# A linear-attention layer and its MoE block on one core: block-diagonal state, wider MoE units, twelve chunks transposed by DMA, every queue's order written out

## The chip, the core and the metric

The kernel runs on one core of a Trainium2 chip. The metric is the device time of one execution in microseconds. Time before: 212.34 us, the median of 3 runs (211.41 to 213.89). The profile is of one execution of its own.

The engines: PE (matrix products, with a separate path for loading weights, PEld), DVE (vector), ACT (scalar functions), POOL (a second vector engine without access to PSUM), and SP, which here only issues DMAs. PSUM, where PE writes, has 8 banks of 512 fp32 columns on each of 128 partitions.

## The reference

```python
def _attn_ref(r, k, v, w, u):          # each (4, 8, 768, 48); u (8, 48)
    state = np.zeros((B, H, D, D))
    for t in range(S):
        cur = np.einsum('bhd,bhe->bhde', u[None] * kt, vt)
        y[:, :, t] = np.einsum('bhd,bhde->bhe', rt, state + cur)
        state = wt[:, :, :, None] * state + np.einsum('bhd,bhe->bhde', kt, vt)
...
def _moe_ref(x, w_in, w_out):          # x (3072, 384), w_in (384, 2048), w_out (2048, 384)
    h = x @ w_in
    r = np.maximum(h, 0.0)
    g = r * r
    return g @ w_out
```

Attention's output y, its heads side by side, is the x of the second part. The output is (3072, 384) in fp32.

## The kernel before, in words

Attention is done in chunks of 128 time steps: 24 of them, 6 to each of the 4 batches. All 8 heads of 48 features lie side by side (384 columns); four pairs of heads share 128 partitions after a transpose, each head padded to 64. A chunk s runs through these helpers (lines are those of the profile):

- load_step (L71): w, r, k and v of the chunk, one DMA of 192 KB each. Rows of one head are 48 fp32 numbers, so the packets have 192 bytes. Seven buffers of each.
- lw_ (ACT, L151) takes log w. cum_ (PE, L178 to L181) makes the column sums of it (four matmuls of one column) and two cumulative sums, one strict for r and one negative and inclusive for k, in two PSUM banks. exp_ (ACT, L186, L187) exponentiates the column sums to a_c, and both cumulative sums in place.
- rd_ (DVE, L191) multiplies r and k by these decays. Eight 128x128 transposes follow, either on PE with a copy by DVE (tr_ L200, rkt_ L204), or, from chunk 18 on (DMA_FROM), as one DMA transpose issued from SP (dtr_, L208).
- p_ (PE, L223) makes the products of k and r for each head, with 64 rows each. pm_ (DVE, L229) masks them in two halves of 512 columns.
- su_ (PE, L238) multiplies decayed k and v for each head, eight matmuls of 48 columns; ts_ (DVE, L245, L247) adds the state S, sn_ (POOL, L251) multiplies by a_c. These tiles have 192 columns: two heads lie one above the other in the partitions.
- y_ (PE, L260, L268) multiplies the masked products by v and r by the state, again head by head, into two banks. ku_, qp_, vq_ (POOL, L159, L163, L171) and q_ (DVE, L167) make the diagonal term with u. ysb_ (DVE, L274) adds it. Three transposes give x transposed in the tile xT: yt_ and xt_ (PE L283, ACT L286), or dyt_ from chunk 18 on (a DMA transpose from SP, L213).

MoE works on blocks of one or two chunks of tokens (14 of them; the blocks of chunks 2, 3, 4 and 23 have one chunk). m1_ (PE, L301) makes one unit of 512 columns in one of two banks; rl_ (ACT, L308) takes 16 * relu to fp16, gt_ (DVE, L313) squares it. m2_ (PE, L320) accumulates an output tile of 128 tokens over 16 matmuls of 384 columns in the only bank for this; os_ (ACT, L325) scales it and store (SP, L329) writes it. Weights come in eight DMAs of 768 KB (L97, L103) and are cast by ACT and DVE (L110). Until MoE has begun, PE runs matmuls on zeros in its gaps (warm_, L334).

The order on every queue is made when the kernel is built: each operation stands in a plan with an engine, an assumed duration, a rank and its inputs, and make_order walks through it in assumed time. The engines then work through their queues in that order, each instruction waiting for its semaphores. So on SP a store or a transpose that waits for its input holds back all loads behind it. The 8 PSUM banks are divided as: two for cumulative sums and products, two for y, one for transposes and state updates, two for m1, one for m2.

Of the kernel before, what the change touches and what calls it, by code (L numbers as in the profile page):

```python
# [9 lines left out]
FP32 = mybir.dt.float32  # L10
FP16 = mybir.dt.float16
# [4 lines left out]

@with_exitstack
def kernel(
# [12 lines left out]
    PSUM = bass.MemoryType.PSUM  # L31

# [9 lines left out]
    NSTEP = B * NCH  # L42
    GW = 512
    RS = 16.0
    A_IN = 7
    HOP = .2
    PACE = 0.0
    DMA_FROM = 18
    LAG = 3.5

    nc.scalar.preload_act_table_set("natural_log_exp_and_others")

    consts = ctx.enter_context(tc.tile_pool(name="consts", bufs=1))
    weights = ctx.enter_context(tc.tile_pool(name="weights", bufs=1))
    stage_pool = ctx.enter_context(tc.tile_pool(name="stage", bufs=8))
    a_in = ctx.enter_context(tc.tile_pool(name="a_in", bufs=A_IN))
    a_mid = ctx.enter_context(tc.tile_pool(name="a_mid", bufs=2))
    a_small = ctx.enter_context(tc.tile_pool(name="a_small", bufs=3))
    gt_pool = ctx.enter_context(tc.tile_pool(name="gt", bufs=3))
    relu_pool = ctx.enter_context(tc.tile_pool(name="relu", bufs=3))  # L60
    o_pool = ctx.enter_context(tc.tile_pool(name="moe_out", bufs=3))

    ps_cp = ctx.enter_context(tc.tile_pool(name="ps_cp", bufs=1, space=PSUM))
    ps_y_pool = ctx.enter_context(tc.tile_pool(name="ps_y", bufs=1, space=PSUM))
    ps_tr_pool = ctx.enter_context(tc.tile_pool(name="ps_tr", bufs=1, space=PSUM))
    ps_m1 = ctx.enter_context(tc.tile_pool(name="ps_m1", bufs=2, space=PSUM))
    ps_m2 = ctx.enter_context(tc.tile_pool(name="ps_m2", bufs=1, space=PSUM))


    def load_one(dst, src, b, c):  # L70
        nc.sync.dma_start(  # L71
            out=dst, in_=src[b, :, c * C:(c + 1) * C, :].rearrange("h c d -> c h d"))

    raw = {}

    def load_step(step, part):
        b, c = divmod(step, NCH)
        if part == "w":
            raw["w", step] = a_in.tile([C, H, D], FP32, name="w_raw")
            load_one(raw["w", step][:], w, b, c)  # L80
        elif part == "r":
            raw["rk", step] = a_in.tile([C, 2, H, D], FP32, name="rk_raw")
            load_one(raw["rk", step][:, 0], r, b, c)
        elif part == "k":
            load_one(raw["rk", step][:, 1], k, b, c)
        else:
            raw["v", step] = a_in.tile([C, H, D], FP32, name="v_raw")
            load_one(raw["v", step][:], v, b, c)

    wi_sb = weights.tile([C, KT, DFF], BF16)  # L90
    wo_sb = weights.tile([C, NT, DM], BF16)
    xT = weights.tile([C, KT, B * S], BF16)
    w_st = {}

    def load_wi(g):
        w_st["i", g] = stage_pool.tile([C, KT, GW], FP32, name="w_st")
        nc.sync.dma_start(  # L97
            out=w_st["i", g][:],
            in_=moe_w_in[:, g * GW:(g + 1) * GW].rearrange("(a p) f -> p a f", p=128))

    def load_wo(g):
        w_st["o", g] = stage_pool.tile([C, 4, DM], FP32, name="w_st")
        nc.sync.dma_start(  # L103
            out=w_st["o", g][:],
            in_=moe_w_out[g * 512:(g + 1) * 512, :].rearrange("(a p) d -> p a d", p=128))

    def cast(eng, kind, g, j):
        dst = wi_sb[:, :, g * GW:(g + 1) * GW] if kind == "i" else wo_sb[:, g * 4:(g + 1) * 4, :]
        copy = nc.scalar.copy if eng == "A" else nc.vector.tensor_copy
        copy(dst[:, j], w_st[kind, g][:, j])  # L110

    u_bc = consts.tile([C, H, D], FP32)

    def load_u():
        nc.sync.dma_start(
            out=u_bc[:],
            in_=bass.AP(tensor=u.tensor, offset=u.offset,
                        ap=[[0, C]] + [list(x) for x in u.ap]))


    tri_strict = consts.tile([C, C], BF16)
    make_upper_triangular(nc, tri_strict[:], val=1.0, diag=False)
    tri_incl_neg = consts.tile([C, C], BF16)
    make_upper_triangular(nc, tri_incl_neg[:], val=-1.0, diag=True)
    ident = consts.tile([C, C], BF16)
    make_identity(nc, ident[:])
    ones_col = consts.tile([C, 1], BF16)
    nc.vector.memset(ones_col[:], 1.0)

    warm = consts.tile([C, 512], BF16)  # L130
    nc.vector.memset(warm[:], 0.0)  # L131

    NLW = 3
    lw_bufs = []
    for i in range(NLW):
        t = consts.tile([C, H, DP], BF16, name=f"lw_buf{i}")
        nc.gpsimd.memset(t[:], 0.0)
        lw_bufs.append(t)
    NRD = 3
    rdec_bufs = []  # L140
    for i in range(NRD):
        t = consts.tile([C, 2, H, DP], BF16, name=f"rdec_buf{i}")
        nc.vector.memset(t[:], 0.0)
        rdec_bufs.append(t)


    tiles = {}

    def lw_(s):
        lw = tiles["lw", s] = lw_bufs[s % NLW]  # L150
        nc.scalar.activation(lw[:, :, 0:D], raw["w", s][:], AF.Ln)  # L151

    def v_(s):
        v_bf = tiles["v", s] = a_mid.tile([C, H, D], BF16, name="v_bf", bufs=3)
        nc.scalar.copy(v_bf[:], raw["v", s][:])  # L155

    def ku_(s):
        ku = tiles["ku", s] = a_mid.tile([C, H, D], FP32, name="ku")
        nc.gpsimd.tensor_mul(ku[:], raw["rk", s][:, 1], u_bc[:])  # L159

    def qp_(s):
        qp = tiles["qp", s] = a_mid.tile([C, H, D], FP32, name="qprod")
        nc.gpsimd.tensor_mul(qp[:], raw["rk", s][:, 0], tiles.pop(("ku", s))[:])  # L163

    def q_(s):
        q = tiles["q", s] = a_small.tile([C, H], FP32, name="q")
        nc.vector.reduce_sum(q[:], tiles.pop(("qp", s))[:], axis=AX.X)  # L167

    def vq_(s):
        vq = tiles["vq", s] = a_mid.tile([C, H, D], FP32, name="vq", bufs=3)  # L170
        nc.gpsimd.tensor_mul(vq[:], raw["v", s][:],  # L171
                             tiles.pop(("q", s))[:, :, None].to_broadcast([C, H, D]))

    def cum_(s):
        lw = tiles.pop(("lw", s))
        cs = tiles["cs", s] = ps_cp.tile([C, 2, 512], FP32, name="cp")
        for p in range(HP):
            nc.tensor.matmul(cs[:, 0, DM + p:DM + p + 1], lw[:, 2 * p:2 * p + 2, :],  # L178
                             ones_col[:], start=True, stop=True)
        nc.tensor.matmul(cs[:, 0, 0:DM], tri_strict[:], lw[:, :, 0:D], start=True, stop=True)  # L180
        nc.tensor.matmul(cs[:, 1, 0:DM], tri_incl_neg[:], lw[:, :, 0:D], start=True, stop=True)  # L181

    def exp_(s):
        cs = tiles["cs", s]
        a_c = tiles["a_c", s] = a_small.tile([C, HP], FP32, name="a_c")
        nc.scalar.activation(a_c[:], cs[:, 0, DM:DM + HP], AF.Exp)  # L186
        nc.scalar.activation(cs[:, :, 0:DM], cs[:, :, 0:DM], AF.Exp)  # L187

    def rd_(s):
        rdec = tiles["rdec", s] = rdec_bufs[s % NRD]  # L190
        nc.vector.tensor_mul(  # L191
            rdec[:, :, :, 0:D], raw["rk", s][:],
            tiles.pop(("cs", s))[:, :, 0:DM].rearrange("p a (h d) -> p a h d", h=H))

    def tr_(s):
        rdec = tiles["rdec", s]
        ps_tr = tiles["tr", s] = ps_tr_pool.tile([C, 2, HP, C], BF16, name="tr")
        for i in range(2):
            for p in range(HP):
                nc.tensor.transpose(ps_tr[:, i, p, :], rdec[:, i, 2 * p:2 * p + 2, :], ident[:])  # L200

    def rkt_(s):
        rkT = tiles["rkT", s] = a_mid.tile([C, 2, HP, C], BF16, name="rkT")
        nc.vector.tensor_copy(rkT[:], tiles.pop(("tr", s))[:])  # L204

    def dtr_(s):
        rkT = tiles["rkT", s] = a_mid.tile([C, 2, HP, C], BF16, name="rkT")
        nc.sync.dma_start_transpose(  # L208
            out=rkT[:].rearrange("p i a t -> p (i a) t"),
            in_=tiles["rdec", s][:].rearrange("t i h d -> t (i h d)"))  # L210

    def dyt_(s):
        nc.sync.dma_start_transpose(  # L213
            out=xT[:, :, s * C:(s + 1) * C],
            in_=tiles.pop(("ysb", s))[:].rearrange("p h d -> p (h d)"))

    def p_(s):
        rkT = tiles["rkT", s]
        ps_p = tiles["p", s] = ps_cp.tile([C, 2, 512], FP32, name="cp")
        for p in range(HP):  # L220
            for e in range(2):
                rows = slice(e * DP, (e + 1) * DP)
# [291 lines left out]
```

## Time and profile before

| what | value |
|---|---|
| median of 3 runs | 212.34 us |
| the profiled execution, its own time | 213.79 us |
| span of that execution, first to last instruction | 212.0 us |
| mean granted clock of PE | 0.992 |
| start of the first MoE matmul | 21.22 us |
| last input load issued | 145.66 us |
| DMA queue: share of 16 engines over the span | 72.6% |
| packets under 512 bytes | 109200 of 116010 |

An engine's busy time is the union of its instructions' times; PE's is pipelined, so that a busy PE need not work at its peak. A wait is put down to what came last. DMA share is the mean busy share of the 16 DMA engines; it can be above 1 in a window when several packets overlap in one engine. A row of a timeline merges successive instructions of one kind: start, length, engine, line, operation, tiles, number.

### The profile page before, as it was taken

How to read it: one execution, taken by the hardware profiler on the slowest of the kernel's cores; microseconds unless marked ns; L12 is line 12 of the kernel's file. 1: busy time of each engine (PE TensorE's matmuls, PEld its weight loads, DVE VectorE, ACT ScalarE, POOL GpSimd, SP SyncE). 2: the span in 40 equal slices, each digit the busy share in tenths (PEclk: the TensorE clock that was granted, in tenths of full speed). 3: DMA queues.
4: the chain of work that ended last, by engine and by line, in shares of the span. 5: the costliest groups of instructions: out<-in, count | busy, mean ns of one | idle time of the engine just before them, and what ended most of it. 6: DMA issues, size and time to landing. Idle time of an engine off the chain costs nothing.

```text
span 212.0 us, 5530 instructions
## 1 busy us (share of the span) xinstructions
PE 194.2 (92%) x2162; PEld 138.1 (65%) x2166; DVE 147.3 (69%) x273; ACT 125.2 (59%) x249; POOL 83.5 (39%) x105
## 2 busy tenths in 40 slices
PE   7897997886999898989989999999999999999983
PEld 3354766554877665767767677777767777777751
DVE  3565795555799798979968999987786666533310
ACT  3353967644666667568477376787645753455530
POOL 5371320545655719747276376363712110000000
PEclk9999999999799999999999999999999999999999
DMA  7999899879975899599978978899444327111111
GB/s 129 202 324 340 200 383 219 170 160 192 181 152 117 174 163 195 107 200 167 178 166 160 204 165 159 155 205 150 101 107 108 62 63 108 56 40 37 39 46 68
DMA packets 116010, 32.61 MB, mean 154 GB/s; under 512 B 109200, under 2 KB 114448, under 8 KB 115984
## 3 DMA queue, kind: packets, MB, share of 16 engines
q1 hardware_dynamic: 115984, 32.25, 72.6%
q8 instruction: 17, 0.28, 0.6%
q14 instruction: 9, 0.07, 0.1%
HBM read 25.36 MB, written 4.72 MB: 142 GB/s over the span
## 4 chain that ended last, share of the span: by engine, by line
PE 44%; DMA 17%; SPq 12%; issue 8%; DVE 8%; POOL 5%; ACT 4%; DVEq 0%; POOLq 0%; ACTq 0%
PE m L320 18%; PE m L301 17%; SPq L71 9%; DMA v_raw<-in_v_dram 6%; DMA w_st<-in_moe_w_out_dram 4%; DMA w_raw<-in_w_dram 3%; DVE gt L313 3%; PE cp L223 2%; POOL qprod L163 2%; DMA rk_raw<-in_r_dram 2%; DVE pmT L229 2%; PE tr L200 2%; ACT o_sb L325 2%; DMA rk_raw<-in_k_dram 2%; SPq L97 1%
## 5 line engine op out<-in xcount | busy, mean ns | idle before, releaser
L301 PE MATMUL m<-xT,wi_sb 128*128 128x256 bf16 (+1 forms) x672 | 77.2, 260 | 3.6 <-ACT xT L286 2.5
L308 ACT ACTIVATE rl<-m 128x512 f16<-128x512 f32 x96 | 56.5, 598 | 39.9 <-PE m L301 39.0
L320 PE MATMUL m<-wo_sb,gt 128*128 128x384 bf16 x384 | 74.8, 326 | 1.8 <-ACT o_sb L325 0.8
L301 PEld LDWEIGHTS <-wi_sb 128*128 128x128 bf16 x672 | 59.0, 99 | 16.8 <-issue 4.7
L313 DVE TENSOR_TENSOR gt<-rl 128x512 bf16<-128x512 f16 x96 | 52.5, 562 | 19.7 <-ACT rl L308 19.5
L320 PEld LDWEIGHTS <-gt 128*128 128x128 bf16 x384 | 35.3, 98 | 20.7 <-DVE gt L313 1.5
L159 POOL TENSOR_TENSOR ku<-rk_raw,u_bc 128x384 f32<-128x384 f32 x24 | 24.3, 1012 | 45.7 <-DMA rk_raw<-in_k_dram 41.1
L229 DVE TENSOR_TENSOR pmT<-cp,tri_strict 128x512 bf16<-128x512 f32 x48 | 30.8, 682 | 4.6 <-PE cp L223 4.4
L191 DVE TENSOR_TENSOR rdec_buf<-rk_raw,cp 128x768 bf16<-128x768 f32 x24 | 22.8, 949 | 13.9 <-ACT cp L187 10.9
L171 POOL TENSOR_TENSOR vq<-v_raw,q 128x384 f32<-128x384 f32 x24 | 21.3, 889 | 15.6 <-DVE q L167 7.6
L163 POOL TENSOR_TENSOR qprod<-rk_raw,ku 128x384 f32<-128x384 f32 x24 | 25.3, 1052 | 1.1
L251 POOL TENSOR_TENSOR S<-t_state,a_c 128x192 bf16<-128x192 f32 x20 | 11.0, 552 | 24.5 <-DVE t_state L247 17.6
L187 ACT ACTIVATE cp<-cp 128x768 f32<-128x768 f32 x24 | 19.1, 797 | 1.0 <-DVE gt L313 0.2
L334 PE MATMUL m<-warm 128*128 128x512 bf16 x60 | 16.8, 409 | 1.3 <-DVE warm L131 1.2
L155 ACT CAST v_bf<-v_raw 128x384 bf16<-128x384 f32 x24 | 12.3, 510 | 9.6 <-DMA v_raw<-in_v_dram 9.2
L151 ACT ACTIVATE lw_buf<-w_raw 128x384 bf16<-128x384 f32 x24 | 12.5, 523 | 7.9 <-DMA w_raw<-in_w_dram 6.1
L167 DVE TENSOR_REDUCE q<-qprod 128x8 f32<-128x384 f32 x24 | 13.1, 546 | 5.3 <-POOL qprod L163 5.3
L325 ACT ACTIVATE o_sb<-m 128x384 f32<-128x384 f32 x24 | 11.8, 492 | 7.7 <-PE m L320 7.0
L274 DVE TENSOR_TENSOR y_sb<-vq,y 128x384 bf16<-128x384 f32 x24 | 13.1, 548 | 3.3 <-PE y L268 3.2
L204 DVE COPY rkT<-tr 128x1024 bf16<-128x1024 bf16 x18 | 12.3, 682 | 1.9 <-PE tr L200 1.9
L200 PE MATMUL tr<-ident,rdec_buf 128*128 128x128 bf16 x144 | 11.5, 225 | 1.2 <-DVE rdec_buf L191 1.0
L223 PE MATMUL cp<-rkT 64*128 64x128 bf16 x192 | 9.7, 221 | 2.1 <-DVE rdec_buf L191 1.9
(40 smaller groups left out, 136.1 us busy)
## 6 DMA issues: line engine op xcount, KB each, us to landing
w_raw<-in_w_dram SPq DMA_DIRECT2D x24, 192.0 KB, 4.3
rk_raw<-in_r_dram SPq DMA_DIRECT2D x24, 192.0 KB, 4.2
rk_raw<-in_k_dram SPq DMA_DIRECT2D x24, 192.0 KB, 4.2
v_raw<-in_v_dram SPq DMA_DIRECT2D x24, 192.0 KB, 4.1
out_dram<-o_sb SPq DMA_DIRECT2D x24, 192.0 KB, 2.0
w_st<-in_moe_w_in_dram SPq DMA_DIRECT2D x4, 768.0 KB, 8.2
w_st<-in_moe_w_out_dram SPq DMA_DIRECT2D x4, 768.0 KB, 8.2
u_bc<-in_u_dram SPq DMA_DIRECT2D x1, 192.0 KB, 4.3
```

Source lines behind the costliest of these rows:

```text
L71: nc.sync.dma_start(out=dst, in_=src[b, :, c * C:(c + 1) * C, :].rearrange("h c d -> c h d"))
L159: nc.gpsimd.tensor_mul(ku[:], raw["rk", s][:, 1], u_bc[:])
L163: nc.gpsimd.tensor_mul(qp[:], raw["rk", s][:, 0], tiles.pop(("ku", s))[:])
L171: nc.gpsimd.tensor_mul(vq[:], raw["v", s][:], tiles.pop(("q", s))[:, :, None].to_broadcast([C, H, D]))
L187: nc.scalar.activation(cs[:, :, 0:DM], cs[:, :, 0:DM], AF.Exp)
L191: nc.vector.tensor_mul(rdec[:, :, :, 0:D], raw["rk", s][:], tiles.pop(("cs", s))[:, :, 0:DM].rearrange("p a (h d) -> p a h d", h=H))
L229: nc.vector.tensor_mul(tiles["pmT", s][:, e], tiles["p", s][:, e].rearrange("p (a t) -> p a t", a=HP), tri_strict[:, None, :].to_broadcast ...
L301: nc.tensor.matmul(ps1[:, j, :], wi_sb[:, kk, n * 128:(n + 1) * 128], xT[:, kk, s0 * C:s0 * C + width], start=(kk == 0), stop=(kk == KT - 1))
L308: nc.scalar.activation(rl[:], tiles.pop(("m1", i, g))[:], AF.Relu, scale=RS)
L313: nc.vector.tensor_mul(tiles["gt", i][:, g * ng:(g + 1) * ng, :], rl[:], rl[:])
L320: nc.tensor.matmul(tiles["m2"][:], gt[:, n, mt * 128:(mt + 1) * 128], wo_sb[:, n, :], start=(n == 0), stop=(n == NT - 1))
L334: nc.tensor.matmul(ps[:], warm[:, 0:C], warm[:], start=True, stop=True)
```

## The change

The kernel is written anew around the same algorithm.

- *State.* S, its update and its product have 384 columns: 96 for a pair of heads, of which each head uses its own half, so that the state is block-diagonal. su and the state part of y are four matmuls of 96 columns on full rows. The zeros outside of the blocks come from am, the exponentials of the column sums written in two halves (ACT), with which POOL multiplies. The column sums moved from cum_ to su and are left out for a batch's last chunk.
- *One output bank.* y has one bank with the heads in order.
- *One cumulative sum.* From chunk 6 on, cum makes only the strict sum for r. ACT writes exp of the sum and of its negative (two operations of 384 columns); ACT also writes 1/w (iw), and POOL multiplies k by it (kd), which takes the place of the inclusive sum. Chunks 0 to 5 (the list TWO) keep two sums.
- *MoE units.* m1 has 1,024 columns in two banks; rl and gt have 1,024 columns. All blocks have two chunks (12 blocks). Output tiles alternate between two banks. The last tile is made, copied and stored in two halves of 192 columns.
- *Masks.* pm is one operation of 1,024 columns.
- *DMA transposes.* Chunks 12 to 23 use dtr and dyt (chunks 18 to 23 before).
- *Buffers.* One tile of 14 slots holds w, r, k, v of a chunk, or one of the eight weight loads. xT is a ring of 12 chunks. u is loaded as one row of 1.5 KB and spread by a matmul (ub, ubc) rather than loaded to 128 partitions.
- *Order.* The planner is gone. A string lists every operation, with the PSUM bank it uses; all queues follow it. Helpers for pairs of chunks are in the file too, and the order has none of them (PAIRS = 0).

The core of the diff:

```diff
+SLOTS = """
+s0:0 s1:1 s2:2 s3:3 i0:4 i1:5 i2:6 i3:7 s4:8 o0:9 o1:10 o2:11 o3:12 s5:13 s6:0 s7:1 s8:2 s9:3 s10:4 s11:5 s12:6 s13:7
+s14:8 s15:9 s16:10 s17:11 s18:12 s19:13 s20:0 s21:1 s22:2 s23:3
+"""
+ORDER = """
+Lk0 Lw0 warm7@7 Lr0 Lv0 lw0 Lw1 cum0@0 warm4@7 ex0 Lk3 rd0 v0 Lr1 tr0@3 lw1 su0@2 rkt0 Lk1 cum1@0 am0 ts0 Lu p0@4 ex1
+warm6@7 Lw3 sn0 pm0 Lw2 y0@2 warm1@7 rd1 ub@3 Lr3 warm3@7 ubc lw3 Lr2 tr1@3 ku0 cum3@0 rkt1 lw2 warm2@7 ku1 Lv4 ex3
+p1@4 warm10@7 pm1 qp0 Lv1 Li0 qp1 rd3 Lk2 q0 cum2@0 q1 tr3@3 Lv2 vq0 ex2 warm4@7 rkt3 ku3 v1 ysb0 p3@4 su1@3 vq1 pm3
+yt0@2 warm3@7 Li3 am1 xt0 qp3 ts1 ciA0.2 y1@2 Lv3 warm3@7 ciA0.1 sn1 ysb1 ciA0.0 q3 yt1@3 ku2 warm4@7 Li2 v4 rd2 xt1
+Li1 v2 qp2 ma0.0@4 q2 tr2@3 rl0.0 vq2 su2@2 rkt2 warm2@7 Lk4 am2 ciV3.1 p2@0 ciV3.2 warm2@7 v3 ciV3.0 ts2 vq3 su3@3
...
+Lk15 p11@0 gt4.2 su12@3 ma4.1@4 am12 pm11 qp14 dtr12 lw15 iw15 ku13 ts12 mb4.0.0@7 v13 st3.1 q14 rl4.1 y11@2 Lw14 kd13
+cum13@0 mb3.0.3 ysb11 ex13 Lr15 ma4.3@4 gt4.1 os3.0 rd13 qp13 yt11@3 mb4.0.1 rl4.3 sn12 Lr16 q13 p12@0 st3.0 kd15 xt11
...
+cum23@0 mb9.0.1 ysb21 ex23 mb9.1.1 dyt21 gt9.2 ma9.3@4 rd23 lw22 iw22 dtr23 cum22@0 ku22 mb9.1.2 rl9.3 mb9.0.2 kd22
+ex22 ma10.0@4 gt9.3 rd22 qp22 mb9.0.3 rl10.0 mb9.1.3 dtr22 q22 os9.0 su22@3 gt10.0 os9.1 p23@0 am22 ma10.1@4 ts22 vq22
+st9.1 pm23 st9.0 sn22 ma10.2@6 rl10.1 gt10.1 p22@0 rl10.2 y23@2 pm22 ma10.3@4 ysb23 gt10.2 y22@3 dyt23 rl10.3
+mb10.1.0@7 ysb22 mb10.0.0@6 gt10.3 dyt22 mb10.1.1 mb10.0.1 mb10.1.2 mb10.0.2 ma11.0@4 mb10.1.3 rl11.0 mb10.0.3 os10.1
+gt11.0 ma11.3@4 os10.0 st10.1 st10.0 ma11.1@6 rl11.3 gt11.3 ma11.2@4 rl11.1 gt11.1 mb11.1.0@7 rl11.2 mb11.0.0@6
...
+"""
+TWO = [0, 1, 2, 3, 4, 5]
+BUFS = {'rd': 4, 'lw': 3, 'rt': 4, 'pm': 3, 'v': 3, 'vq': 4, 'ys': 3, 'qp': 2, 'st': 3, 'rl': 3, 'gt': 3, 'o': 3}
...
+    def Lu():
+        nc.sync.dma_start(out=u_row[:], in_=bass.AP(tensor=u.tensor, offset=u.offset, ap=[[0, 1], [1, DM]]))
...
+    def iw(s):
+        nc.scalar.activation(single(s)[:, 0], buf(lw_b, s)[:, :, 0:D], AF.Exp, scale=-1.0)
+
+    def kd(s):
+        nc.gpsimd.tensor_mul(single(s)[:, 0], single(s)[:, 2], single(s)[:, 0])
...
+    def cum(s, bank):
+        if s in TWO:
+            nc.tensor.matmul(ps[:, bank, 0:DM], tri[:], buf(lw_b, s)[:, :, 0:D], start=True, stop=True)
+            nc.tensor.matmul(ps[:, bank + 1, 0:DM], ntri[:], buf(lw_b, s)[:, :, 0:D], start=True, stop=True)
+        else:
+            nc.tensor.matmul(ps[:, bank + 1, 0:DM], tri[:], buf(lw_b, s)[:, :, 0:D], start=True, stop=True)
...
+    def ex(s):
+        bank = held["cp", s]
+        if s in TWO:
+            nc.scalar.activation(ps[:, bank:bank + 2, 0:DM], ps[:, bank:bank + 2, 0:DM], AF.Exp)
+        else:
+            nc.scalar.activation(ps[:, bank, 0:DM], ps[:, bank + 1, 0:DM], AF.Exp, scale=-1.0)
+            nc.scalar.activation(ps[:, bank + 1, 0:DM], ps[:, bank + 1, 0:DM], AF.Exp)
...
+    def pm(s):
+        bank = held["p", s]
+        nc.vector.tensor_mul(buf(pm_b, s)[:].rearrange("p e a t -> p (e a) t"),
+                             ps[:, bank:bank + 2].rearrange("p e (a t) -> p (e a) t", t=C),
+                             tri[:, None, :].to_broadcast([C, 8, C]))
+
+    def su(s, bank):
+        for a in range(HP):
+            nc.tensor.matmul(ps[:, bank, a * 96:a * 96 + 96], buf(rd_b, s)[:, 1 - ri(s), 2 * a:2 * a + 2, :],
+                             buf(v_b, s)[:, 2 * a:2 * a + 2, :], start=True, stop=True)
+        for a in range(HP):
+            nc.tensor.matmul(ps[:, bank, DM + a:DM + a + 1], buf(lw_b, s)[:, 2 * a:2 * a + 2, :],
+                             ones[:], start=True, stop=True)
...
+    def am(s):
+        bank = held["su", s]
+        for e in range(2):
+            rows = slice(e * DP, (e + 1) * DP)
+            nc.scalar.activation(buf(am_b, s)[rows, :, e], ps[rows, bank, DM:DM + HP], AF.Exp)
...
+    def sn(s):
+        nc.gpsimd.tensor_mul(buf(st_b, s + 1)[:].rearrange("p (a e d) -> p a e d", a=HP, e=2),
+                             buf(ts_b, s)[:].rearrange("p (a e d) -> p a e d", a=HP, e=2),
+                             buf(am_b, s)[:, :, :, None].to_broadcast([C, HP, 2, D]))
...
+        if s % NCH:
+            for a in range(HP):
+                nc.tensor.matmul(ps[:, bank, a * 96:a * 96 + 96], rt1(s)[:, HP * ri(s) + a, :],
+                                 buf(st_b, s)[:, a * 96:a * 96 + 96], start=False, stop=True,
+                                 skip_group_check=True)
...
+    def rl(i, g):
+        bank = held["m1", i, g]
+        t = held["rl", i, g] = buf(rl_b, unit0[i] + g)
+        nc.scalar.activation(t[:], ps[:, bank:bank + 2].rearrange("p b n -> p (b n)"), AF.Relu, scale=RS)
+
+    def gt(i, g):
+        t = held.pop(("rl", i, g))
+        nc.vector.tensor_mul(buf(gt_b, i)[:, g * 1024:(g + 1) * 1024], t[:], t[:])
```

In the string, L followed by w, r, k or v is a load, Li and Lo are weight loads, ci and co casts (A on ACT, V on DVE), ma and mb the two MoE stages (block, unit or tile, quarter), os and st the output copy and store; the number after @ is the bank.

## The prediction

> **What bounds the kernel now.** I read the page first: engine shares, the 40 slices, the chain by engine. Then the windows by stage, then the waits, then the timeline around the first MoE matmul, the transposes and the end.
>
> ```profile
> PE 194.2 (92%) x2162; PEld 138.1 (65%) x2166; DVE 147.3 (69%) x273; ACT 125.2 (59%) x249; POOL 83.5 (39%) x105
> ...
> PE   7897997886999898989989999999999999999983
> ...
> DMA  7999899879975899599978978899444327111111
> ...
> PE 44%; DMA 17%; SPq 12%; issue 8%; DVE 8%; POOL 5%; ACT 4%; DVEq 0%; POOLq 0%; ACTq 0%
> ```
>
> PE is the fullest engine, and from the 28th slice (about 145 us) it has no gap, while DMA falls away there. Up to there DMA is just as full, and the chain mixes both. So there are two regimes: a front that the loads feed, and a back that is a backlog of MoE on PE.
>
> ```profile
> 0.00:60.00 60.00, 51.39 (x531) 33.49 (x536) 37.65 (x74) 34.02 (x68) 24.46 (x38) 0.97 0.96 226
> 60.00:140.00 80.00, 75.25 (x945) 55.66 (x945) 71.52 (x123) 52.70 (x110) 48.06 (x53) 1.00 0.88 165
> 140.00:185.00 45.00, 44.57 (x502) 32.49 (x500) 31.88 (x64) 27.15 (x52) 10.95 (x14) 1.00 0.52 104
> 185.00:212.00 27.00, 22.99 (x191) 16.44 (x189) 6.28 (x15) 11.32 (x20) 0.00 (x0) 1.00 0.13 45
> ```
>
> Columns after the length: busy PE, PE weight loads, DVE, ACT, POOL, granted clock, DMA share. PE idles 8.6 us in the first 60 us (DMA share 0.96) and 4.8 us from 60 to 140 (DVE 89% busy there). The loads end at about 150 us and 55 us of PE work are left.
>
> ```profile
> 21.22 1.47 PE L301 MATMUL m<-xT,wi_sb 128*128 128x256 bf16 x12 [1.04 <-ACT xT L286]
> ```
>
> ```profile
> 130.27 0.33 PE cp L223 x8
> 130.60 0.55 PE tr L200 x8
> 131.15 0.65 PE m L320 x4
> 131.80 0.66 PE m L301 x6
> ```
>
> The first fence, of the timeline, is the start of MoE. The second, rows of the chain (start, us, what), is the price list of PE when dense: 0.33 us for the products of a chunk, 0.55 for its eight transposes, 0.163 for a second-stage matmul, 0.109 for a first-stage one. By the timeline of the end, the last output tile waits 0.58 us (205.26 to 205.81) for its only bank.
>
> **PE before, as a sum.** MoE is 576 x 0.109 (a 128-column one counts half: twelve of them take 0.67) plus 384 x 0.163 = 125.4 us. Attention, from successive starts in the timeline at 142 to 151 us: two cumulative sums 0.33, column sums 0.11, products 0.33, state update 0.24, y 0.30, state part of y 0.20, transposes of y 0.17, of r and k 0.55. With 24, 24, 24, 20, 24, 20, 18 and 18 of them: 47.4. Total 172.8. The two chunks ahead of the first MoE matmul hold 4.2 of it. So 21.2 + 168.6 + 3.4 (last matmul to end) = 193.2, and 18.8 us of the 212.0 are idle, warm-up and slack after MoE began: about 10 before 60 us (6.2 idle, ten warm-up matmuls 2.1, and a clock of 0.83 in 50 to 60, 1.7), about 9 later.
>
> **What the change takes from PE.** 18 chunks with one cumulative sum: 18 x 0.16 = 2.9. Six more chunks transposed by DMA: 6 x (0.55 + 0.17) = 4.3. Block-diagonal state: 4 matmuls of 96 columns for 8 of 48, twice per chunk. No row has 96 columns. By columns it is 96/256 x 0.109 = 0.04 each, 0.16 for 0.24 and 0.20, a gain of 2.8 with the four dropped column sums (0.44); by the transposes of 128 columns it is 0.55/8 = 0.07 each, 0.28, a loss of 2.0. The eight matmuls of y, as full in rows and 48 wide, take 0.0375 each, so I stay near the columns: 0.045, a gain of 2.0. The MoE columns stay. Sum 9.2, PE total 163.6.
>
> **Start.** The first weights now come after 14 input loads, not 9. Under load an input load takes 1.0 to 1.1 us (issues spaced 0.95 to 1.1 us at 50 to 56 us); u shrinks to one row and saves one. In the trace the first weights were cast from 14.2 us on, so now at about 18.5, and 1.7 us of casts make it 20.2. The last of the 14, v of chunk 1, lands at about 17, and v in bf16, vq, y and its transposes put xT of chunk 1 at about 20 too. First MoE matmul 21 to 23, I take 22, but with 5.6 us of attention done rather than 4.2 (the order has chunks 0 and 1, the sums, transposes and products of 3 and the sums of 2 ahead of it). Left on PE: 158.0. **End.** Two output banks and a last tile in halves remove the 0.58 wait and a part of the copy (0.49): 3.4 becomes 3.2. Sum without idle: 22 + 158.0 + 3.2 = 183.2.
>
> **What idle stays.** The front is fed by the same bytes at share 0.96; of the 10 us there I keep 8. Later, against 9 us, several things move.
>
> DMA: 12 transposed chunks rather than 6.
>
> ```profile
> L208 SPq DMA_TRANSPOSE rkT<-rdec_buf x6: 1232/1237/2128, 142.2 to 174.0; - x6
> ```
>
> ```profile
> SPq L329 <- ACT o_sb L325: 50.9, 18, 4.9
> SPq L213 <- DVE gt L313: 11.6, 4, 4.0
> ```
>
> The first fence is the transpose of r and k: shortest, median and longest issue in ns; it lands 3.3 us after its issue, one of y 2.3. The second is the two largest of SP's own waits (us, times, longest): stores wait for their copies, transposes for DVE, and every load behind them waits too. Summing the DMA share by single microseconds between 155 and 189 us, a transpose of r and k costs about 1.45 us of all DMA engines (2.1 in 161 to 165, less 0.6 for the store in it), one of y 0.49. Six more chunks: 11.7 us. Shares up to 150 us sum to 138 us; less 13 stores and two transposes that is 127 for all loads. When the last transpose of r and k is issued in the new order, the queue has moved 126 + 18 x 0.6 + 11 x 1.45 + 10 x 0.49 = 158 us of DMA work. At share 1.04 (10 to 20 us) that is 154 us of clock, at the average 0.92 it is 174. PE work behind it is 24 us, which with the end puts the finish at 181 to 201. So DMA is nearly as tight as PE until the last chunks. The 14 input slots (7 before) let loads run further ahead, which is the cover.
>
> POOL: k times the inverse decay, 18 x 1.0; the state product has 384 elements for 192: between 0.55 and 0.89 each (rows of 192 and 384), I take 0.85, +6. Total 83.5 to about 107, 62% of the first 170 us; no bound. DVE: rkT -4, wider ts +4, mask product in one (1.29 for the pair, I take 1.2) -2, gt 48 x (0.75 free to 1.1) for 52.5: 129 to 146 against 147. ACT: inverse decay 18 x 0.52, split exp and am +6.5, wider rl -7, xT -3: about 131, 67%; no bound. A unit of 1,024 columns (1.31 on PE) frees its banks only after rl of 1.03 (0.176 for 4 columns, 0.598 for 512, so by the slope); between two units PE has on average two second-stage groups (1.3) and 0.8 of attention, so it is covered unless two ACT operations stand ahead.
>
> The row that speaks against it: gt takes 408 ns at best and 1,237 at worst, and the long ones lie beside POOL products.
>
> ```profile
> L313 DVE TENSOR_TENSOR gt<-rl x96: 408/425/1237, 22.8 to 203.2; 128x512 bf16<-128x512 f16 x96
> ```
>
> ```profile
> 121.77 1.85 DVE L313 TENSOR_TENSOR gt<-rl 128x512 bf16<-128x512 f16 x2
> ...
> 122.15 1.19 POOL L163 TENSOR_TENSOR qprod<-rk_raw,ku 128x384 f32<-128x384 f32 x1
> ```
>
> The excess over 0.42 is 52.5 - 40.3 = 12 us now; POOL is busy 49% of the first 170 us now and 62% then, so 12 x 62/49 = 15, on an engine with a tenth to spare. The Trainium skill (SBUF — State Buffer, Summary) says that a DVE operation with two SBUF inputs and a GpSimd operation that reads SBUF exclude each other, the second blocking fully; the rows agree. By it, an estimate of 48 x 0.62 x 0.5 us = 15.
>
> The Trainium skill (Advanced Engine Details and Errata, X-Bar Transpose) holds transposing DMAs as fast as regular ones. The rows differ: 256 KB in 1.45 us against 192 KB of a store in 0.6. By the rule six more chunks would cost an estimated 6.6 us, not 11.7, and the lower end would be 5 us earlier.
>
> So of the later 9 us I keep 6: coarser units, the DMA squeeze and gt give back part of what the tuned order could win. Span 183.2 + 8 + 6 = 197.2. The profiled execution took 213.79 for a span of 212.0; 197.2 + 1.8 = 199.0 is 0.931 of it, and of the median 212.34 that is 198.
>
> **Rivals.**
> 1. SP becomes the bound (slower). In chunks 12 to 22 SP issues per chunk 4 loads x 0.7 + 1.24 + 1.18 + a store 0.4 = 5.6 us, in order. PE's turn per chunk is 125.4/24 + 1.4 = 6.6. In the trace 12 transposes waited 26 us on SP (the row above, 6.2, 4.4 and 4.0), 2.2 each, with almost no load behind them. If they wait so with loads behind, a turn is 10 us and eleven turns lose 37. For: these waits, and 50.9 us at stores. Against: 14 slots, and the order can put a transpose where its input is ready. It ends slower once a transpose waits over 1.2 us on average (8.0 per turn, +15); I price it at 1.5: 198 + 11 x 2.0 = 220, less some prefetch, 216.
> 2. DVE and POOL hold each other: +8 us in the middle (60 to 140 is at 89% already): 206.
> 3. The order fits, and only the front's 8 us stay idle: 183.2 + 8 = 191.2 of span, 192.
> 4. DMA keeps its average of 0.92 and paces everything, and gaps of 7 to 10 us add up behind it: 201 + 9 = 210 to 213, no change.
>
> **Chances.** Forecast (194 to 202) 0.42; rival 3 0.18; rival 2 0.20; rival 4 0.07; rival 1 0.13. One per cent is about what a measurement of this kernel can tell from none: faster 0.82, same 0.05, slower 0.13. The range leaves out rival 1 and the lowest part of rival 3: 189 to 210; the forecast's own is 194 to 202.
>
> **What would show it.** Right: MoE starts at 21 to 23 us; PE has about 9 us less to do; the tail after the last matmul is near 3.2; DMA stays near 0.9 to 160 us and beyond; POOL near 107 busy. Rival 1: the chain full of SP between 90 and 165 us and DMA share well under 0.9 there. Rival 2: gt means over 1.1 us and DVE as releaser of PE's gaps. Wrong altogether: PE gaps of over 1 us before first-stage units, put down to rl, which would mean that the 1,024-column unit is too coarse for its one pair of banks.

## The result, and the profile after

The changed kernel takes 197.09 us (median of 4 runs, 195.81 to 197.90) against 213.12 us (4 runs) for the kernel before beside it: a ratio of 0.927 [0.917, 0.936]. A second measurement gave 196.97 us and 0.9223 [0.9192, 0.9253]. The forecast was 198 us. The profiled execution took 196.81 us for a span of 194.9 us, at a granted clock of 1.00.

The engines' shares, the slices and the chain by engine, from the page of the kernel after:

```profile
PE 182.9 (94%) x1823; PEld 129.6 (66%) x1823; DVE 140.1 (72%) x203; ACT 127.3 (65%) x249; POOL 110.7 (57%) x120
...
PE   6999988999998799899999999999998989999993
...
DMA  6999999996698999697998997799797799382202
...
q1 hardware_dynamic: 123794, 34.22, 83.7%
...
PE 55%; DVE 14%; DMA 8%; ACT 6%; issue 4%; SPq 1%; DVEq 0%; ACTq 0%
```

PE idles 12.0 us (194.9 - 182.9) where it idled 17.8, and does 11.3 us less. DMA no longer falls away at 145 us: input loads are issued until 162 us (145.7 before), and with the transposes they keep it full to about 165. SP has 1% of the chain (12% before), DMA half its former share, DVE nearly twice. The old border between a fed front and a dense back is gone.

The same windows as before, with the last one cut at the new end (columns: busy PE, PE weight loads, DVE, ACT, POOL, clock, DMA share, GB/s):

```profile
0.00:60.00 60.00, 56.05 (x501) 34.64 (x503) 43.47 (x75) 37.54 (x74) 28.93 (x40) 1.00 0.91 230
60.00:140.00 80.00, 76.54 (x833) 56.91 (x832) 66.98 (x88) 60.00 (x122) 63.23 (x62) 1.00 0.94 178
140.00:185.00 45.00, 43.45 (x435) 32.73 (x434) 27.54 (x39) 26.59 (x48) 18.52 (x20) 1.00 0.75 135
185.00:195.00 10.00, 6.84 (x63) 5.29 (x60) 2.08 (x3) 3.20 (x5) 0.00 (x0) 1.00 0.12 42
```

Idle of PE up to 60 us went from 8.6 to 4.0, although MoE starts later (23.33 us, 21.22 before); 60 to 140 went from 4.8 to 3.5. POOL has 63 of 80 us in the middle (48 before).

PE's timeline: the start of MoE, and the prices of y (masked products times v) and of the state part behind it.

```profile
23.33 1.47 PE L516 MATMUL ps<-xT,wi_sb 128*128 128x256 bf16 x12
...
54.15 0.36 PE L367 MATMUL ps<-v,pm 128*128 128x48 bf16 x8
54.35 0.33 PE L371 MATMUL ps<-st,rt 128*128 128x96 bf16 x4
54.52 0.33 PE L291 MATMUL ps<-lw,tri 128*128 128x384 bf16 x1
```

A row's own length overlaps the next, so prices are read between starts: eight matmuls of y cost 0.20 us, the four of the state 0.17. Before they stood so, in a chunk with a state part and then in the first chunk of a batch, which has none:

```profile
121.72 0.36 PE L260 MATMUL y<-v_bf,pmT 128*128 128x48 bf16 x8
122.02 0.27 PE L268 MATMUL y<-S,rkT 64*128 64x48 bf16 x8
122.22 0.34 PE L283 MATMUL tr<-ident,y_sb 128*128 128x128 bf16 x3
...
151.28 0.36 PE L260 MATMUL y<-v_bf,pmT 128*128 128x48 bf16 x8
151.48 0.24 PE L178 MATMUL cp<-ones_col,lw_buf 128*128 128x1 bf16 x4
```

So y fell from 0.30 to 0.20, which I had not priced, and the state part from 0.20 to 0.17. Without a state part behind it, y took 0.20 before as well, into the same two banks. The difference lies in its last matmul: the step from it to the next start is 0.115 us in all 20 chunks where matmuls on 64 rows (64*128) follow, and 0.025 in the four where matmuls on 128 rows do. The groups of relu and square in the page after (busy us, mean ns, idle before and its releaser):

```profile
L523 ACT ACTIVATE rl<-ps 128x1024 f16<-128x1024 f32 x48 | 49.0, 1023 | 24.7 <-PE ps L516 23.7
...
L527 DVE TENSOR_TENSOR gt<-rl 128x1024 bf16<-128x1024 f16 x48 | 42.4, 887 | 20.9 <-ACT rl L523 20.4
```

The square takes 42.4 us instead of 52.5, in half the operations.

### The profile page after: what moved, and what is told of

It is laid out like the page before. It is cut to its first block, busy times and chain, and to the rows that moved or that the text cites. A ratio compares the mean times of both kernels' runs of the same rounds, so it can differ in the third digit from the quotient of the medians.

```text
span 194.9 us, 4703 instructions
## 1 busy us (share of the span) xinstructions
PE 182.9 (94%) x1823; PEld 129.6 (66%) x1823; DVE 140.1 (72%) x203; ACT 127.3 (65%) x249; POOL 110.7 (57%) x120
## 3 DMA queue, kind: packets, MB, share of 16 engines
q1 hardware_dynamic: 123794, 34.22, 83.7%
## 4 chain that ended last, share of the span: by engine, by line
PE 55%; DVE 14%; DMA 8%; ACT 6%; issue 4%; SPq 1%; DVEq 0%; ACTq 0%
PE ps L542 23%; PE ps L516 21%; DMA rt<-rd 5%; DVE gt L527 3%; PE ps L326 3%; DVE rd L304 3%; DVE pm L332 2%; PE ps L367 2%; DMA raw<-in_r_dram 2%; PE ps L371 1%; DVE ts L356 1%; DVE ys L377 1%; DMA raw<-in_v_dram 1%; PE ps L312 1%; PE ps L291 1%
## 5 line engine op out<-in xcount | busy, mean ns | idle before, releaser
L516 PE MATMUL ps<-xT,wi_sb 128*128 128x256 bf16 x576 | 70.0, 273 | 1.6 <-DVE wi_sb L242 0.8
L542 PE MATMUL ps<-wo_sb,gt 128*128 128x384 bf16 (+1 forms) x400 | 70.9, 320 | 0.3 <-DVE gt L527 0.3
L523 ACT ACTIVATE rl<-ps 128x1024 f16<-128x1024 f32 x48 | 49.0, 1023 | 24.7 <-PE ps L516 23.7
L516 PEld LDWEIGHTS <-wi_sb 128*128 128x128 bf16 x576 | 55.0, 98 | 11.7 <-DVE wi_sb L242 1.4
L527 DVE TENSOR_TENSOR gt<-rl 128x1024 bf16<-128x1024 f16 x48 | 42.4, 887 | 20.9 <-ACT rl L523 20.4
L270 POOL TENSOR_TENSOR qp<-raw,u_bc 128x384 f32<-128x384 f32 x24 | 27.0, 1128 | 11.3 <-DMA raw<-in_k_dram 8.5
L332 DVE TENSOR_TENSOR pm<-ps,tri 128x1024 bf16<-128x1024 f32 x24 | 29.2, 1218 | 5.6 <-PE ps L326 5.6
L359 POOL TENSOR_TENSOR st<-ts,am 128x384 bf16<-128x384 f32 x20 | 18.7, 937 | 22.8 <-DVE ts L354 8.3
L273 POOL TENSOR_TENSOR qp<-raw,qp 128x384 f32<-128x384 f32 x24 | 26.6, 1111 | 3.4 <-DMA raw<-in_r_dram 2.9
L279 POOL TENSOR_TENSOR vq<-raw,q 128x384 f32<-128x384 f32 x24 | 20.7, 862 | 13.3 <-DVE q L276 13.3
L304 DVE TENSOR_TENSOR rd<-raw,ps 128x768 bf16<-128x768 f32 x24 | 22.8, 949 | 6.4 <-ACT ps L297 2.5
L551 ACT ACTIVATE o<-ps 128x384 f32<-128x384 f32 (+1 forms) x25 | 11.7, 476 | 8.8 <-PE ps L542 8.7
```

The source lines that it names most:

```text
L270: nc.gpsimd.tensor_mul(buf(qp_b, s)[:], single(s)[:, 2], u_bc[:])
L273: nc.gpsimd.tensor_mul(buf(qp_b, s)[:], single(s)[:, 1], buf(qp_b, s)[:])
L279: nc.gpsimd.tensor_mul(vq_b[:, s % BUFS["vq"]].rearrange("p (h d) -> p h d", h=H), single(s)[:, 3], buf(q_b, s)[:, :, None].to_broadcast([ ...
L304: nc.vector.tensor_mul(buf(rd_b, s)[:, :, :, 0:D], single(s)[:, x:x + 2], ps[:, bank:bank + 2, 0:DM].rearrange("p a (h d) -> p a h d", h=H))
L332: nc.vector.tensor_mul(buf(pm_b, s)[:].rearrange("p e a t -> p (e a) t"), ps[:, bank:bank + 2].rearrange("p e (a t) -> p (e a) t", t=C), t ...
L359: nc.gpsimd.tensor_mul(buf(st_b, s + 1)[:].rearrange("p (a e d) -> p a e d", a=HP, e=2), buf(ts_b, s)[:].rearrange("p (a e d) -> p a e d", ...
```

## The experiments

The theory on trial was the one of my forecast: PE's work plus the gaps that remain sets the end. The rivals: DMA or SP paces the kernel; DVE and POOL hold each other; and, as it turned out, the order rather than the parts is what gains. Ratios are to runs of the kernel before on the same chip, with 95% intervals.

| run | us, median | ratio to before |
|---|---|---|
| after, again | 196.97 | 0.9223 [0.9192, 0.9253] |
| e1: two cumulative sums again | 197.21 | 0.9229 [0.9196, 0.9263] |
| e2: chunks 12 to 17 transposed by PE | 203.41 | 0.9503 [0.9464, 0.9542] |
| e3: relu and square in halves | 209.40 | 0.9797 [0.9767, 0.9827] |
| e8: relu alone in halves | 197.09 | 0.9262 [0.9198, 0.9325] |
| e9: square alone in halves | 208.94 | 0.9778 [0.9685, 0.9871] |
| e5: after, long load rows | 194.72 | 0.9107 [0.9043, 0.9170] |
| e6: before, long load rows | 208.31 | 0.9739 [0.9677, 0.9802] |
| e4: before, DMA transposes from chunk 12 | 220.32 | 1.0283 [1.0203, 1.0364] |
| e10: before, wide square | 216.78 | 1.0173 [1.0110, 1.0237] |
| e7: all parts of after, order by the old planner | 211.49 | 0.9879 [0.9780, 0.9977] |
| e11: as e7, DMA transposes from chunk 18 | 209.68 | 0.9843 [0.9778, 0.9908] |

**The change once more (a0).**

> The changed kernel as it is, as the yardstick of this group: 197 us, 0.92 to 0.94 of the kernel before, by every theory.

It measured 196.97 us, as expected.

**e1: the inclusive sum back on PE.**

```diff
-TWO = [0, 1, 2, 3, 4, 5]
+TWO = list(range(24))
 # ORDER: every iw and kd taken out
```

> Two cumulative sums in all chunks; the inverse decay (ACT, 18 x 0.52) and its product with k (POOL, 18 x 1.03) are gone. Theory (PE work sets the end): PE gets 18 x 0.16 = 2.9 us more, so about 200 us, although POOL falls by 18 and ACT by 13. Rival (DVE, POOL and ACT feed PE too slowly): no slower than the changed kernel, 193 to 197.

```profile
PE 185.8 (95%) x1841; PEld 131.7 (67%) x1841; DVE 138.8 (71%) x203; ACT 118.3 (60%) x213; POOL 90.9 (46%) x102
```

PE is busy 2.9 us longer, exactly as priced, and the time does not move (+0.2 us, the intervals lie on each other): the rival's range came, not my 200 us. POOL has 19.8 us less and ACT 9.0 less, the mean square falls from 887 to 832 ns, and PE's idle time from 12.0 to 10.2 us. What PE saves by the single sum, PE gives back in gaps. As part of this order, that edit is worth nothing, and a sum of PE's work alone does not forecast it.

**e2: six chunks transposed by PE again.**

```diff
 # ORDER, for each chunk N of 12 to 17, at the same place
-dtrN
+trN@b rktN
-dytN
+ytN@b xtN
```

> Chunks 12 to 17 transposed by PE, at the place in the order where the DMA transposes stood. Theory (PE work): PE gets 6 x (0.45 + 0.18) = 3.8 us more, so about 201 us, although the DMA queue has 11.7 us less to do. Rival (DMA or SP paces the second half): faster than the changed kernel, 190 to 196.

It costs 6.4 us (203.41 against 196.97). PE is busy 4.9 us more (187.8), and its idle time grows from 12.0 to 14.3 us: the copies are back on DVE and ACT, in an order that was written without them. The windows of e2:

```profile
0.00:60.00 60.00, 56.05 (x496) 34.56 (x497) 43.13 (x75) 37.23 (x74) 28.72 (x39) 1.00 0.90 229
60.00:140.00 80.00, 73.96 (x825) 55.94 (x823) 63.27 (x88) 58.11 (x120) 56.01 (x55) 1.00 0.69 141
```

The DMA share from 60 to 140 us falls from 0.94 to 0.69, yet PE is busy 2.6 us less in this stretch. That refutes DMA or SP as what paces this order.

**e3, e8, e9: halves again.** MoE units stay at 1,024 columns; relu, square or both go in two operations of 512.

```diff
-        nc.scalar.activation(t[:], ps[:, bank:bank + 2].rearrange("p b n -> p (b n)"), AF.Relu, scale=RS)
+        for b in range(2):
+            nc.scalar.activation(t[:, b * 512:(b + 1) * 512], ps[:, bank + b], AF.Relu, scale=RS)
...
-        nc.vector.tensor_mul(buf(gt_b, i)[:, g * 1024:(g + 1) * 1024], t[:], t[:])
+        for b in range(2):
+            cols = slice(b * 512, (b + 1) * 512)
+            nc.vector.tensor_mul(buf(gt_b, i)[:, g * 1024:(g + 1) * 1024][:, cols], t[:, cols], t[:, cols])
```

> Units of 1,024 columns on PE as they are, but relu and square each in two operations of 512. ACT gets 48 x (2 x 0.598 - 1.023) = 8.3 us more. Theory (PE work): hidden, 196 to 199 us. Rival (ACT and DVE near the path, the wide operations are the gain): 201 us or more.

> The changed kernel with only relu in two operations of 512 columns (ACT +8 us); the square stays at 1,024. Theory formed after the first runs (what halving costs is DVE: every square is one more operation that POOL can lock out): 197 to 199 us. Rival (the longer turn on ACT, whose end frees the banks): 203 or more.

> The changed kernel with only the square in two operations of 512 columns; relu stays at 1,024. Theory (DVE and the lock): DVE about 17 to 20 us busier, 205 to 209 us. Rival (ACT's turn): 197 to 199.

All 12 us come from the square (e9: 208.94); the relu in halves is neutral (e8: 197.09). My first theory, which had e3 hidden at 196 to 199 us, was wrong; the ranges for e8 and e9, written after it, came. The tile of the squares, in after and then in e3 (shortest, median and longest ns):

```profile
L527 DVE TENSOR_TENSOR gt<-rl x48: 675/693/1490, 29.1 to 187.6; 128x1024 bf16<-128x1024 f16 x48
```

```profile
L530 DVE TENSOR_TENSOR gt<-rl x96: 407/426/1245, 29.5 to 200.2; 128x512 bf16<-128x512 f16 x96
```

In e3 the squares keep DVE busy for 63.4 us in place of 42.4. By the medians 96 x 0.426 - 48 x 0.693 = 7.6 of these 21.0 us is the plain cost of more operations; the other 13.4 is length that single ones gain. In after, the 16 squares with no POOL operation beside them take 675 to 693 ns, the 32 others up to 1,490; in e3 it is 407 to 426 for 38, and up to 1,245 for 58. The timeline of e3 shows where:

```profile
99.26 1.00 POOL L273 TENSOR_TENSOR qp<-raw,qp 128x384 f32<-128x384 f32 x1
99.29 4.65 DVE L530 TENSOR_TENSOR gt<-rl 128x512 bf16<-128x512 f16 x4
...
100.21 1.18 POOL L270 TENSOR_TENSOR qp<-raw,u_bc 128x384 f32<-128x384 f32 x1
...
101.35 1.18 POOL L264 TENSOR_TENSOR raw<-raw 128x384 f32<-128x384 f32 x1
...
102.49 1.17 POOL L273 TENSOR_TENSOR qp<-raw,qp 128x384 f32<-128x384 f32 x1
...
103.87 1.21 DVE L332 TENSOR_TENSOR pm<-ps,tri 128x1024 bf16<-128x1024 f32 x1
...
105.13 0.37 PE L367 MATMUL ps<-v,pm 128*128 128x48 bf16 x8 [2.42 <-DVE pm L332]
...
105.73 1.49 PE L545 MATMUL ps<-wo_sb,gt 128*128 128x384 bf16 x4
...
107.01 2.46 PE L516 MATMUL ps<-xT,wi_sb 128*128 128x256 bf16 x12
```

Four squares take 4.65 us, 1.16 each, the very step of the POOL operations (1.14 between their starts, 1.00 when undisturbed): the two engines alternate, one operation each. The mask product behind them is late, and PE stands for 2.42 us. A wide square pays such a turn at most once per 1,024 columns (1.49 - 0.69 = 0.80), a halved one twice. This is what the Trainium skill (SBUF — State Buffer, Summary: rules for kernel authors) describes as the second one blocking until the first is done; the rows agree with it.

The last two rows show a second cost. Four second-stage matmuls take 1.28 us between starts where they take 0.65 elsewhere: for 3.4 us from 105.6 us the granted clock is half. Such a stretch stands at 71.5 us too, and after has none. An estimate is 1.7 us for each, half its length. In e9 the execution at a clock of 0.999 took 206.81 us, and two at 0.982, which is two such stretches, 208.66 and 209.22. So about 2 of the 12 us go with the clock. How much of the other 10 is the lock and how much an order written for other durations, these runs do not part.

**e5, e6: loads with rows of 1,536 bytes.** Inputs are read as contiguous rows, so other elements land in the tiles; the number of bytes stays.

```diff
+ in_=bass.AP(tensor=src.tensor, offset=src.offset + s * C * DM, ap=[[DM, C], [1, DM]])
```

> The changed kernel with the input loads of w, r, k and v reading as many bytes in rows of 1,536 bytes (other elements than the reference's, so the output is not the reference's). It shows how much of the time the short packets hold. Theory (PE work, with a front fed by DMA): MoE starts about 4 us earlier and idle in the front goes, 187 to 191 us. Rival (DMA paces all of it): 183 or less. Rival (DMA is hidden throughout): 195 or more.

> The kernel before with the same edit of its loads (output not the reference's). Theory: its front idles 10 us and starts MoE late for the same reason, 202 to 206 us. Rival (its gaps came from its order and banks, not from DMA): 209 or more.

```profile
q1 hardware_dynamic: 37778, 34.22, 64.0%
```

The queue of e5 has less than a third of the packets and 64.0% of the span instead of 83.7%, and the kernel gains 2.3 us, 1.1 of it in the start of MoE (22.26 for 23.33 us). I had expected 187 to 191 us; 194.72 lies by the rival's 195, of a hidden DMA. The kernel before gained 5.5 us, less than I expected too (202 to 206). So the old one was paced by loads in part, as its chain said, and the new one hardly is.

**e4: the DMA transposes alone, in the kernel before.** One number, `DMA_FROM` 18 to 12; the planner makes the order anew.

> The kernel before with one constant changed: DMA transposes from chunk 12 on, its own planner ordering all. Theory (PE work): PE has 3.8 us less, so 209 to 210 us. Rival (the DMA queue, 92% full up to 150 us, and SP in order): the same or slower, 213 to 220.

```profile
PE 31%; DMA 27%; SPq 15%; DVE 9%; ACT 7%; issue 6%; POOL 3%; ACTq 0%; DVEq 0%; POOLq 0%
```

6.5 us slower, just past the rival's range; my theory had it faster. The same edit that is worth 6.4 us in the new kernel (e2) costs as much in the old one. Here DMA and SP take 42% of the chain (29% before), SP's waits ahead of transposes grow from 26.2 to 31.7 us, and the loads of w go from 3% to 12% of the chain. That fits transposes that hold back loads behind them in SP's queue; it was not tried apart. The trace also has two stretches at half clock where before has one, an estimated 1.7 us.

**e10: the wide square alone, in the kernel before.** One relu tile for two units, one square of 1,024 columns per two units, planned at 0.75 us.

> The kernel before with units of 512 columns and relu as they are, but one square of 1,024 columns for two units, ordered by its own planner. Theory (DVE is near the path between 60 and 140 us, where it is 89% busy): DVE 8 to 10 us less busy, 207 to 211 us. Rival (only the wide unit on PE and ACT helps, or the second stage waits longer for its square): 213 or more.

```profile
PE 195.0 (91%) x2162; PEld 138.3 (65%) x2166; DVE 134.6 (63%) x225; ACT 125.1 (58%) x249; POOL 86.3 (40%) x105
```

DVE falls from 147.3 to 134.6 us, and the kernel is 1.7% slower; my theory had it faster. A part that the new order cannot do without (e9) gains nothing in the old one. Why is not shown. The edit makes each square wait for the second relu, but PE's waits for squares hardly change (0.9 us, 0.7 before); its waits for the decayed r and k grow from 2.9 to 5.5 us, and there are two stretches at half clock (one before).

**e7, e11: all parts, the old order.** The tiles, operations and buffers of after, but every queue in the order that the old planner's rules make (its assumed costs set to the new operations, its ranks and other settings unchanged); e11 with DMA transposes from chunk 18, so with the parts of e2. The order string also names the PSUM bank of each operation, and the planner's choice differs there: all 48 units in one pair of banks, where the written order puts 8 in the other pair.

> All parts of the change, ordered by the planner of the kernel before with new durations (loads in chunk order, one pair of banks for units, two for output tiles). Theory (parts 9 us on PE and the tail, order about half of the rest): 203 to 206 us. Rival (the order is all of the gain): 210 to 214. Rival (the order is worth nothing): 196 to 198.

> The same parts as the run with chunks 12 to 17 transposed by PE, but ordered by the planner of the kernel before. The two differ in the order alone. Theory (half of the gain is the order): 207 to 210 us, against 203.4 with the written order. Rival (the parts are enough, the DMA transposes spoiled the other planned run): 202 to 205. Rival (the order is nearly everything): 211 or more.

e7 at 211.49 us came in the rival's range, e11 in the one I expected. e11 is 209.68 us, e2 with the same parts 203.41: the order, with the banks it names, is worth 6.3 us by the medians, 7.3 by the ratios. The windows of e11, to be held against those of e2:

```profile
0.00:60.00 60.00, 52.42 (x462) 32.73 (x466) 40.53 (x72) 36.24 (x70) 30.66 (x40) 0.97 0.88 224
60.00:140.00 80.00, 74.53 (x855) 56.69 (x852) 67.43 (x92) 58.46 (x121) 68.25 (x68) 1.00 0.85 178
```

The planner starts MoE at 19.73 us, 3.6 earlier than the written order, and still has less done at 60 us: 105 matmuls of the first stage and 60 of the second against 119 and 64. What PE waited for in e11 (us in all, times, longest):

```profile
PE ps L542 <- DVE gt L527: 3.1, 6, 0.9
PE ps L516 <- ACT rl L523: 2.8, 4, 1.6
```

In e2 these two are 0.3 and 1.6 us. The chain of e11 runs through POOL for 22% of the span, that of e2 for 6%. The clock of 0.97 is one stretch at half clock in e11 (an estimated 1.7 of the 6 to 7 us); e2 has none. With the planner, DMA transposes from chunk 12 rather than 18 bring nothing (211.49 against 209.68, intervals overlap); with the written order they bring 6.4. So the 16 us part as: about 3 from the parts under the old order (e11), 6 to 7 from the order (e11 to e2), 6 from the transposes, which of the two orders only the written one can use (e2 to after). The shares hang on this path: the string was written for all the parts at once, so e2 and e9 take a part out of an order made for it. Whether a better tuned planner would close some of this was not tried.

## Why the forecast was right, point by point

The time was right, and so was the mechanism in outline (less work for PE, fewer gaps). Several terms were wrong and cancelled; that the sum came within 1 us is in part luck.

- *Single cumulative sum, 2.9 us.* PE's work fell by as much (e1), the time by nothing. What PE gains goes in gaps; that POOL's 18 products and ACT's inverse decays make them by way of DVE is likely (the mean square is 55 ns longer with them) and was not tried apart. The step that failed is "what the change takes from PE" used as time.
- *Six more chunks by DMA, 4.3 us.* Worth 6.4 (e2). The price of eight transposes was misread: a row of the chain counts from end to end, and gave 0.55. Between starts it is 0.46 in the median of the 18 before (26.44 to 26.88 us for one) and 0.45 after, so PE's share is 3.7. What came on top is gaps.
- *Block-diagonal state, 2.0 us.* The 96-column matmul takes 0.043, I took 0.045: the size was right, by luck, and the reason was not the columns. In both traces, at full clock, every step from a matmul on 128 rows to one on 64, or back, is 0.09 to 0.10 us longer than a step from the same matmul without such a change. The old state part took 0.20 with 128 rows behind it, and only 0.115 the two times that products on 64 rows followed, less than the new one's 0.167. What full rows save is these changes. One of them stood at the end of y: 20 x 0.09 = 1.8 us that I did not see. The banks of y have no part in it, as its first chunks show.
- *PE in all.* 163.6 less 1.8 and 12 x 0.10 (transposes) is about 160.5; 5.3 of it lies ahead of MoE.
- *Start and end.* MoE began at 23.33, I said 22 and at most 23. The last matmul row ends at 191.85 (below), 3.05 us before the end; I said 3.2.

```profile
182.61 3.93 PE ps L516 x36
186.54 5.31 PE ps L542 x48
```

- *Idle that stays, 8 and 6.* With these numbers 194.9 - 23.3 - 3.05 - (160.5 - 5.3) leaves 13.4 us for idle, warm-up and slack after MoE began; I had 14. The split was wrong: to 60 us it is about 4 (1.5 idle, twelve warm-ups 2.6, no clock lost where before lost 1.7), later about 9. "The front is fed by the same bytes" was the failed step: the new order gave 4 us back there under a DMA share of 0.91 (0.96 before).
- *"Coarser units give back part".* Not borne out where it was tried: the wide relu is neutral (e8), the wide square is what the order lives from (e9). PE's unit of 1,024 columns itself stayed in all these runs. I had the excess of gt at 15 us; it is 48 x (0.887 - 0.69) = 9.5, fewer operations having fewer turns to lose. My named sign of failure, gaps over 1 us before first-stage units put down to rl, did not come (0.8 us in all).
- *DMA "nearly as tight as PE".* The queue's time rose by only 163.1 - 153.9 = 9.2 us from before to after, since other transfers got cheaper. The six chunks themselves cost more: e2, with six fewer, has 69.6% of 202.1, 140.7 us, so they took 22.4. By the trace's packets of 256 bytes, which are the transposes, six chunks took 11.7 us before and 11.5 in e2, as I had priced them, and twelve took 33.4 in after. So six more cost nearly twice my 11.7, and the Trainium skill's rule (Advanced Engine Details and Errata, X-Bar Transpose), with its estimated 6.6, lies further off. Still the queue was not tight: with over two thirds of the packets gone the kernel gained 2.3 us (e5). In the sum of clock time, 158/1.04 and 158/0.92 are 152 and 172, 2 us less than I wrote.
- *"14 slots are the cover".* Wrong. Counted in the written string, never more than 6 of the 14 hold data between a load's issue and its last use. Loads are issued just in time, so what covers the transposes must be where they stand; that was not tried apart.
- *Rival 1 (SP).* Refuted by the time, 197 us and not 216. SP's 1% of the chain is weaker evidence: in e1, as fast, it has 18%. The transposes did wait, as in the two largest of their waits here (SP's own; us, times, longest), about 1.6 us each over 24, more than the 1.2 that I had named as the limit. What failed is the step from these waits to lost time.

```profile
SPq L391 <- DVE ys L377: 9.1, 4, 4.4
SPq L391 <- DVE gt L527: 7.5, 6, 2.1
```

- *Rival 2 (DVE and POOL).* Its mechanism is real and is the nearest to a bound: e3 shows it full size, at a price of 12 us (clock and order included) rather than 8. In after it is held small by the wide square.
- *Rival 3 and 4.* The later gaps did not vanish (about 9 us), and DMA does not pace (e2, e5).

What stands after all this: no engine alone bounds the kernel after. The end is set by PE's queue in its order and by many small gaps in it. DVE's turns make part of them, longer where POOL runs beside (e3, e9); the arrival of transposes makes others (1.5 us). Open are the parting of the other 10 us of e9, why six more chunks of transposes cost the queue nearly twice as much as the first six, and whether e1's parts would gain with an order of their own.

## What to carry to other kernels

Price an edit on the engine that it relieves and on those that it loads: 2.9 us off the fullest engine were worth nothing here, since POOL and ACT got 29 us in exchange. The sign of a part can hang on the order it stands in (DMA transposes: +6.5 us in one order, -6.4 in another), so try a part in the order that it will have. Where DVE runs operations with two SBUF inputs beside a busy POOL, make them few and long, and order the rest for it: alone it gained nothing (e10). Count how often PE goes from matmuls on full rows to ones on half the rows, not only their columns.

## What the runs showed of the hardware that I had not expected

A change between matmuls on 128 and on 64 rows cost PE 0.09 to 0.10 us each time: a first-stage matmul's step is 0.109 us to the next of its kind and 0.205 to the products of a chunk. The DMA transpose of r and k landed later in the fuller queue: issue to landing, shortest, median and longest in after, against 3.3 us before.

```profile
L319 SPq DMA_TRANSPOSE rt<-rd x12: 1231/1289/2728, 91.9 to 169.2; - x12
...
DMA to landing us min/median/max: 3.1/4.2/5.3
```

Two of them stand in the chain that ended last, 9.8 us in all, a latency that a sum of DMA work doesn't contain. PE itself stood idle for them for only 1.5 us:

```profile
144.12 4.46 DMA rt<-rd
...
154.61 5.32 DMA rt<-rd
```
